# First batch attended in two row parts, w_out scaled by halves, some low halves of w_in by TensorE

## The chip, the cores and the metric

One NeuronCore of a Trainium2 chip runs the whole program. The metric is the device time of one execution in microseconds (us), the median of the runs. Five engines work side by side, each with its own queue of instructions in program order: PE (TensorE, matrix products into PSUM; PEld are its weight loads), DVE (VectorE), ACT (ScalarE), POOL (GpSimd), and SP, which here only issues DMAs. PSUM has eight banks of 128 x 512 fp32.

## The reference

Causal attention over 4 batches, 12 heads, 448 rows of 64, and then an MLP with a squared relu over the 1792 rows of 768:

```python
scores = scale * np.matmul(q, k.transpose(0, 1, 3, 2))       # [4, 12, 448, 448]
scores = np.where(mask, -1000000000.0, scores)               # causal
scores = scores - np.max(scores, axis=-1, keepdims=True)
attn = np.exp(scores)
attn = attn / (np.sum(attn, axis=-1, keepdims=True) + 1e-09)
attn_out = np.matmul(attn, v).astype(np.float32)
x = attn_out.transpose(0, 2, 1, 3).reshape(1792, 768)
h = x @ w_in                                                 # w_in  [768, 2048], float64
r = np.maximum(h, 0.0)
g = r * r
return (g @ w_out).astype(np.float32)                        # w_out [2048, 768], float64
```

q, k and v are float32. The two weights arrive as float64, 12.6 MB each.

## The kernel before

**Arithmetic.** A float32 factor is split into a high and a low f16 half, and a product is three f16 products (high-high, high-low, low-high) accumulated in PSUM. Powers of two, worked out on the chip from sums of squares, keep the halves in range (`pow2`, lines 439 to 452). Batch 0's whole attention and the scores of batch 1 are done in fp32 instead; the scores of batches 2 and 3 and all other products with the attention weights are split.

**Attention** (`pair`, 598 to 758). A batch has 6 pairs of heads. A pair's q and k are turned to have d on the partitions (for batches 0 and 1 by PE with the identity, 629, and a copy, 577; for 2 and 3 by splitting, 416 to 430, and a DMA transpose, 614). Rows go in 4 chunks of 112; chunk c has scores for c + 1 key blocks. `soft` (647) scales, masks and takes the row's extremum on DVE in one custom operation (649, which leaves a second small instruction that reads the accumulator) and takes the exponential and its row sum on ACT (653). Batch 0 then scales the weights (`scaled`, 569), turns them block by block on PE (709), copies them (577) and multiplies with v in fp32 (721). Batches 1 to 3 split them into `psrc` (`halves`, 583: 416/418 high, 429 low), a DMA transpose brings them to `pT` (595), and PE multiplies (731). x goes to `xt` in two halves (748, 752). The low half of a block, in any place, is a DVE operation on a scaled difference (429) or two POOL operations; an unscaled one is line 424.

**Weights** (`weights_in`, 826; `weights_out`, 865). w_in comes in 24 tiles of 128 x 512, w_out in 16 of 128 x 768. Each is staged as raw float64 in whatever lies free (g, xt of odd batches, `raw`), narrowed to float32 bit by bit (`narrow`, 793), and squared by PE for its scale (840, 881). Narrowing is two DVE operations (801, 804) and a third that adds the low word: on DVE too (809), or, in every second tile (`POOLED`), a conversion on ACT (815) and an add on POOL (817), in pieces of 512. w_in gets a scale for each of four column groups `f`; w_out gets its scale from all of its 16 tiles and the four scales of w_in. Then `split_w` (820) writes the halves over the float32. The raw q, k and v of batch 0 lie in the space of w_out from its tile 5 on.

**MLP** (`sub_block`, 931). The 1792 rows go in sub-blocks of 256 or 128 rows: batch 0 has 256 and 128 (its last 64 rows are handled with batch 1), batch 1 has 256 and 256, and so on. A sub-block first rescales x by powers of two (940 to 966, all six pairs), then for 16 column blocks `m` runs 18 products over w_in (L1, 996), relu (1007, ACT), square (1014), high half (416) and low half (424, POOL or DVE). Then for each 128 rows and each half of the 768 output columns it runs 48 products over all of w_out (L2, 1032), one eviction with a scale per row on ACT (1042), and a DMA out (1046).

**Order.** All of this is listed as operations with the tiles that they read and write. `Plan` (69 to 260) puts them in order: it plays a list schedule with the estimated length of each operation on each engine that may do it, and of the operations that are ready it picks the one with the smallest due time, which is a number per phase and per kind from the table `PR` (21). Operations with several possible engines (high halves, squares, copies, scalings) are given one there. Phases are a0 to a3 (attention), m (MLP), wi/ws (w_in narrowed / split), wo/wt (w_out). In the list of the program, attention 0 comes first, then the weights, then for each batch its MLP and the attention of the next.

PSUM banks are given out by role: pv in 0; scores of batch 0 in 1, 3 and 2, 4, of batch 1 in 1 and 2; transposes in 5, 6 or 3; L1 in 4 and 5; L2 in 6 and 7; sums of squares in 7.

Of the kernel before, what the change touches and what calls it, by code (L numbers as in the profile page):

```python
# [68 lines left out]
class Plan:  # L69
# [26 lines left out]
    def spot(self, keys, ap):  # L96
# [190 lines left out]
def dma_ns(nbytes, run):  # L287
    return nbytes / (360.0 if run >= 512 else 180.0)
# [3 lines left out]
def attention_relu2_kernel(  # L292
# [37 lines left out]
    F16V = [False, True, True, True]  # L330
# [180 lines left out]
    def v_up(b):  # L511
        return vst[:, 8 * (b % 2) + 6:8 * (b % 2) + 7]
# [352 lines left out]
    def weights_out():  # L865
        for i in range(KF):
# [7 lines left out]
            if i == 0:  # L874
                ps = n_gram()
# [253 lines left out]
```

## Time and profile before

| | |
|---|---|
| median of 3 runs | 677.19 us (676.54 to 678.2) |
| the profiled execution | 677.23 us |
| its span, first to last instruction | 675.5 us |
| PE busy | 618.0 us |
| ACT busy | 439.4 us |
| DVE busy | 380.3 us |
| POOL busy | 153.3 us |
| mean granted TensorE clock | 0.96 |

The busy time of PE says how long products were in it, not how fast it went: the granted clock has two levels, 1.2 and 2.4 GHz, and is given as a share of the full one, as a mean over a stretch. A product at half clock counts twice the time. So a stage is read by two numbers together, busy time and clock.

### The profile page before, as it was taken

The numbers are of one execution on the slowest core, as the hardware profiler recorded it, in microseconds if no ns is written. First come the engines' busy times: TensorE is split into PE (matmuls) and PEld (weight loads), VectorE is DVE, ScalarE is ACT, GpSimd is POOL, SyncE is SP. The second block draws the span as 40 slices with busy tenths as digits, with TensorE's granted clock in tenths as the row PEclk, the third lists the DMA queues.
The fourth block names the chain that finished last, engine by engine and source line by source line (L and its number), as shares of the span: only waits on it lengthen the run. The fifth ranks groups of instructions, "written<-read, shape, count | busy, mean of one in ns | idle before, by whom it ended". The sixth has DMA issues, their size and how long they took to land.

```text
span 675.5 us, 13694 instructions
## 1 busy us (share of the span) xinstructions
PE 618.0 (91%) x5030; PEld 448.6 (66%) x5030; DVE 380.3 (56%) x1134; ACT 439.4 (65%) x1275; POOL 153.3 (23%) x202
## 2 busy tenths in 40 slices
PE   5876766689999998999999999999999999999997
PEld 3444545366676575778686687768777778767864
DVE  3999898989897766966878777750200300200000
ACT  2878878789999797788877996744514434304400
POOL 4332223103321231143001323112302122103200
PEclk9987778779999998999999999999999999999999
DMA  9998767667655899878999997681000000000000
GB/s 245 304 274 249 250 236 277 151 150 131 144 94 104 178 180 187 174 124 168 183 183 167 186 182 131 127 162 40 13 13 24 14 13 1 13 24 13 13 25 23
DMA packets 208675, 87.30 MB, mean 129 GB/s; under 512 B 196064, under 2 KB 203488, under 8 KB 208608
## 3 DMA queue, kind: packets, MB, share of 16 engines
q1 hardware_dynamic: 208608, 86.43, 56.6%
q8 instruction: 39, 0.64, 0.4%
q14 instruction: 28, 0.23, 0.1%
HBM read 45.81 MB, written 5.51 MB: 76 GB/s over the span
## 4 chain that ended last, share of the span: by engine, by line
PE 58%; DMA 14%; DVE 12%; ACT 10%; issue 3%; SPq 2%; POOL 1%; POOLq 0%; ACTq 0%; DVEq 0%
PE bank L1032 25%; PE bank L996 22%; DMA pT<-psrc 4%; PE bank L731 3%; PE bank L666 3%; DVE bank L649 2%; ACT p L653 2%; DVE wi L804 2%; PE bank L680 2%; ACT psrc L416 2%; DMA qT<-qs 1%; ACT p L569 1%; DMA vn<-in_v_dram 1%; DMA raw<-in_moe_w_in_dram 1%; DVE psrc L429 1%
## 5 line engine op out<-in xcount | busy, mean ns | idle before, releaser
L996 PE MATMUL bank<-xt,wi 128*128 128x256 f16 (+1 forms) x2304 | 232.4, 260 | 0.9 <-ACT r L1007 0.9
L1032 PE MATMUL bank<-wo,g 128*128 128x384 f16 x1344 | 230.4, 327 | 0.0
L996 PEld LDWEIGHTS <-wi 128*128 128x128 f16 x2304 | 201.2, 98 | 27.7 <-issue 5.2
L1032 PEld LDWEIGHTS <-g 128*128 128x128 f16 x1344 | 130.4, 98 | 84.4 <-issue 3.8
L424 POOL TENSOR_TENSOR g<-g,g 128x256 f16<-128x256 f32 (+1 forms) x128 | 83.8, 667 | 290.3 <-ACT g L416 183.6
L653 ACT ACTIVATE p<-bank,nm 112x112 f32<-112x112 f32 (+3 forms) x192 | 93.1, 489 | 28.2 <-DVE nm L649 23.0
L429 DVE SCALAR_TENSOR_TENSOR psrc<-p,nm,psrc 112x112 f16<-112x112 f32 (+3 forms) x144 | 70.8, 518 | 11.4 <-ACT psrc L416 10.6
L1007 ACT ACTIVATE r<-bank 128x256 f32<-128x256 f32 (+1 forms) x128 | 44.6, 354 | 50.1 <-PE bank L996 49.1
L1042 ACT ACTIVATE ob<-bank,fac 128x384 f32<-128x384 f32 x28 | 16.2, 578 | 84.3 <-PE bank L1032 84.3
L416 ACT ACTIVATE psrc<-p,nm 112x112 f16<-112x112 f32 (+3 forms) x144 | 65.4, 520 | 6.5 <-DMA pT<-psrc 6.0
L951 DVE TENSOR_SCALAR u<-bank 128x256 int32<-128x256 int32 (+1 forms) x8 | 3.1, 382 | 106.0 <-PE bank L946 106.0
L649 DVE CUSTOM_DVE_ANT_0 bank<-bank,mask,sc 112x112 f32<-112x112 f32 (+3 forms) x96 | 48.2, 511 | 15.0 <-PE bank L666 7.8
L416 ACT ACTIVATE g<-g 128x256 f16<-128x256 f32 (+1 forms) x128 | 47.2, 388 | 12.7 <-PE bank L1032 11.4
L1014 ACT ACTIVATE g<-r 128x256 f32<-128x256 f32 (+1 forms) x128 | 49.3, 386 | 8.4 <-POOL g L424 4.9
L680 PE MATMUL bank<-kT,qT 64*112 64x336 f32 (+3 forms) x192 | 39.5, 480 | 10.6 <-ACT p L653 7.9
L649 DVE CUSTOM_DVE_ANT_0 bank<-bank,mask 112x112 f32<-112x112 f32 (+3 forms) x96 | 40.9, 476 | 11.3 <-PE bank L680 8.1
L666 PE MATMUL bank<-kT,qT 128*112 128x112 f16 (+3 forms) x192 | 36.3, 288 | 2.1 <-ACT p L653 1.9
L653 ACT ACTIVATION_READ_ACCUMULATOR p<-bank,nm 112x1 f32 x192 | 38.3, 199 | 0.0
L709 PE MATMUL bank<-ident,p 112*112 112x112 f32 x120 | 28.6, 393 | 7.7 <-ACT p L569 5.1
L731 PE MATMUL bank<-pT,vp 112*64 112x448 f16 (+3 forms) x432 | 30.2, 284 | 4.6 <-DMA pT<-psrc 3.7
L731 PEld LDWEIGHTS <-vp 112*64 112x64 f16 x432 | 22.0, 109 | 15.2 <-issue 7.0
L680 PEld LDWEIGHTS bank<-kT,qT 64*112 64x112 f32 x192 | 16.4, 188 | 20.9 <-ACT p L653 14.1
(120 smaller groups left out, 669.0 us busy)
## 6 DMA issues: line engine op xcount, KB each, us to landing
raw<-in_moe_w_out_dram SPq DMA_DIRECT2D x8, 768.0 KB, 5.1
xt<-in_moe_w_out_dram SPq DMA_DIRECT2D x8, 768.0 KB, 5.6
xt<-in_moe_w_in_dram SPq DMA_DIRECT2D x11, 512.0 KB, 5.3
out_dram<-ob SPq DMA_DIRECT2D x28, 192.0 KB, 1.9
raw<-in_moe_w_in_dram SPq DMA_DIRECT2D x9, 512.0 KB, 6.0
vn<-in_v_dram SPq DMA_DIRECT2D x18, 224.0 KB, 3.1
raw<-in_v_dram SPq DMA_DIRECT2D x18, 224.0 KB, 3.3
raw<-in_q_dram SPq DMA_DIRECT2D x12, 224.0 KB, 3.5
```

The lines of the kernel that those rows point to most:

```text
L416: nc.scalar.activation(out=o, in_=i, func=ACTF.Copy, scale=s)
L424: return plan.add({"dve": dve_ns(n), "pool": pool2_ns(n)}, lambda e: engines[e].tensor_tensor(out=out(), in0=in_(), in1=top(), op=ALU.subt ...
L429: nc.vector.scalar_tensor_tensor(out=out(), in0=in_(), scalar=scale(), in1=top(), op0=ALU.mult, op1=ALU.subtract)
L649: one("dve", dve_ns(w, 1, 2 if F16S[b] else 1) - 10, lambda e: nc.vector.tensor_tensor_reduce(out=s.ap[0:P, 0:w], in0=s.ap[0:P, 0:w], in1= ...
L653: one("act", act_ns(w, True, 1, True), lambda e: nc.scalar.activation(out=p32[j].ap[:, b0:b0 + c + 1, :].rearrange("p a t -> p (a t)"), in ...
L666: nc.tensor.matmul(out=s.ap[0:P, 0:(c + 1) * P], lhsT=qT.ap[:, j * NCH + c, :], rhs=kT.ap[:, a:a + c + 1, :].rearrange("p a t -> p (a t)") ...
L680: nc.tensor.matmul(out=ss[j].ap[0:P, 0:(c + 1) * P], lhsT=f32t(q32)[r, c * P:(c + 1) * P], rhs=f32t(k32)[r, 0:(c + 1) * P], start=True, st ...
L731: nc.tensor.matmul(out=pv.ap[j * D:(j + 1) * D, kc * P:S], lhsT=vp.ap[:, hv, vb:vb + D], rhs=pT[j].ap[0:P, hp * NSL + x:hp * NSL + x + w, ...
L996: nc.tensor.matmul(out=h.ap[:, 0:n], lhsT=wi_hl(ci, hw)[:, ms], rhs=x[:, kd, hx, off:off + n], start=(kd == 0 and hw == 0 and hx == 0), st ...
L1007: nc.scalar.activation(out=r.ap[:, 0:n], in_=h.ap[:, 0:n], func=ACTF.Relu)
L1014: nc.scalar.activation(out=g32.ap[:, 0:n], in_=r.ap[:, 0:n], func=ACTF.Square)
L1032: nc.tensor.matmul(out=o.ap[:, 0:HALF], lhsT=g[:, kf, hg, tt * 128:(tt + 1) * 128], rhs=wo_hl(kf, hw)[:, hh * HALF:(hh + 1) * HALF], start ...
```

## The change

Batch 0 is attended by a function of its own, `early`, in two row parts: part 0 is rows 0 to 255 in two chunks of 128, part 1 is rows 256 to 447 in two chunks of 96. Each part goes through all six pairs, the scores of a pair ahead of the weights and values of the pair before it, with three sets of buffers in turn (some of them in psrc, which is therefore padded later). Its q and k are turned in one group per pair and copied back in place. The program's list is now: part 0, w_in, part 1, w_out, then both sub-blocks of batch 0, with both first layers (L1) ahead of both second layers (L2), and batch 1's attention after them. The second sub-block has a g of its own in the space of qT and kT.

w_out is scaled in two halves of 8 tiles, each with its own scale, so L2 runs in two accumulations of 24 products; ACT evicts the first, DVE adds the second to it. All tiles are narrowed by three DVE operations. For the first two of four column groups of w_in (12 tiles) the low half is made by PE: diag(scale) times the float32 tile, less the high half, and a copy out of PSUM. Batch 1's q and k are copied in place, its scores have two banks per head, those of batches 2 and 3 three. All of PR's numbers differ, and two more phases, e (part 1) and n (MLP of batch 0), have their own; the estimate of DMA lengths is lower.

```diff
-    POOLED = (1, 3, 5, 7)
-    SB = {True: ([1, 3], [2, 4]), False: ([1], [2])}
-    TB = {True: [5, 6], False: [3]}
-    HB = {True: [4, 5], False: [4, 5]}
-    OB = {True: [6, 7], False: [6, 7]}
+    SB = {0: ([1, 3], [2, 4]), 1: ([1], [2])}
+    TB = {0: [5, 6], 1: [3]}
+    HB = [4, 5]
+    OB = [[6, 4, 5], [6, 7]]
-    S16 = [1, 2]
+    S16 = [1, 2, 3]
+    S32 = ([1, 3], [2, 7])
+    WL = [6]
+    ON_PE = 2
+    KEYS = [(0, 128), (128, 128), (256, 96), (352, 96)]
...
+    EARLY = [(n, part, c) for n in range(3) for part in range(2) for c in range(2)]
+    early_at = lambda n, part, c=0: wo[:, (5 + 4 * n + 2 * part + c) * 2 * DM:(6 + 4 * n + 2 * part + c) * 2 * DM].bitcast(F32)
...
-        plan.add({"act": act_ns(n, False, 1), "dve": dve_ns(n, 1, 1), "pool": pool_ns(n, 1)}, fn, reads, writes, due, "nrm", True)
+        plan.add({"act": act_ns(n, False, 1), "dve": dve_ns(n, 2, 1), "pool": pool_ns(n, 1)}, fn, reads, writes, due, "nrm", True)
...
+    def early(part):
+        T0, M, N = (0, 128, 256) if part == 0 else (256, 96, 192)
+        phase, slot = ("a", 2) if part == 0 else ("e", 0)
...
+        def scored(pr):
...
+            one("pe", 4 * (0.86 * M), turn, qkk + ["ident"], [t], due)
+            copy(4 * M, lambda rows=rows: rows[:, :, part, :, 0:M],
+                 lambda t=t: t.ap[:, 0:4 * M].rearrange("p (n c t) -> p n c t", n=2, c=2), [t], qkk, due)
+            p32, pT = [[mk(j) for j in range(2)] for mk in (lambda j: n_ep(part, j, pr % 3), lambda j: n_eT(j, pr % 3))]
...
+        for step in range(NPAIR + 1):
+            if step < NPAIR:
+                scored(step)
+            if step:
+                applied(step - 1)
...
+    def split_pe(src, hl, n, key, scale, skey, dg, due):
+        hi(n, lambda: hl(0), lambda: src, scale, [key(1), skey], [key(0)], due)
+        t = n_wl()
+
+        def rest(e):
+            nc.tensor.matmul(out=t.ap[:, 0:n], lhsT=dg.ap, rhs=src, start=True, stop=False)
+            nc.tensor.matmul(out=t.ap[:, 0:n], lhsT=minus, rhs=hl(0), start=False, stop=True)
+
+        one("pe", mm32_ns(n) + mm_ns(n), rest, [key(1), key(0), dg, "minus"], [t], due)
+        plan.add({"act": act_ns(n, True), "dve": dve_ns(n)}, lambda e:
+                 nc.scalar.activation(out=hl(1), in_=t.ap[:, 0:n], func=ACTF.Copy) if e == "act"
+                 else nc.vector.tensor_copy(out=hl(1), in_=t.ap[:, 0:n]), [t, key(1)], [key(0)], due, "rest")
...
-            pr, z = divmod(i + 1 - 5, 2)
-            over = [k_ for n in (z, z + 1) for k_ in raw_of(pr)[n][1]] if 0 <= pr < NPAIR else []
+            over = [("b0", *EARLY[i - 4], pr) for pr in range(NPAIR)] if 4 <= i else []
...
+            if i % (KF // 2) == KF // 2 - 1:
+                scale_out(i // (KF // 2), ps)
...
+            if z == 0:
+                ob = held[tt, hh] = n_ob(phase == "n" and n == SUB, 2 * tt + hh)
+                one("act", act_ns(HALF, True, 1), lambda e: nc.scalar.activation(
+                    out=ob.ap, in_=o.ap[:, 0:HALF], func=ACTF.Copy, scale=scale()),
+                    [o, (facs[tt], 1)], [ob], (phase, pos, "ob"))
+                return pos
+            ob = held[tt, hh]
+            one("dve", dve_ns(HALF, 1, 1), lambda e: nc.vector.scalar_tensor_tensor(
+                out=ob.ap, in0=o.ap[:, 0:HALF], scalar=scale(), in1=ob.ap, op0=ALU.mult, op1=ALU.add),
+                [o, (facs[tt], 2), ob], [ob], (phase, pos, "ob"))
...
+    early(0)
+    weights_in()
+    early(1)
+    weights_out()
+    pos, last0 = sub_block(0, 0, 256, 0, [(256, 2)], 0.0, "n")
+    pos, last1 = sub_block(0, 256, 128, 256, [(128, 0)], pos, "n", True)
+    last1(last0(pos))
+    spare = [plan.spot([("psrc", i, j) for j in range(2)], psrc[i]) for i in range(2)]
+    plan.add({"pool": 2000}, pads, [], spare + ["pads"] + [("psrc", i, c, z) for i in range(2) for c in range(NCH) for z in range(2)],
              ("a", H, "ld"))
-    attention(0)
-    weights_in()
-    weights_out()
+    attention(1)
     pos = 0.0
-    for b in range(B):
+    for b in range(1, B):
```

## Rows read from the trace of the kernel before

**Rows 1.** The page, busy time by engine: us, share of the span, instructions

```profile
PE 618.0 (91%) x5030; PEld 448.6 (66%) x5030; DVE 380.3 (56%) x1134; ACT 439.4 (65%) x1275; POOL 153.3 (23%) x202
```

**Rows 2.** Stretches from:to us: length, busy us by engine, granted clock, DMA

```profile
0.00:20.00 20.00, 11.65 (x58) 6.63 (x58) 8.01 (x32) 6.38 (x17) 8.27 (x11) 1.00 1.01 261
20.00:143.00 123.00, 88.32 (x572) 58.31 (x571) 116.16 (x323) 98.92 (x270) 33.71 (x27) 0.80 0.79 242
143.00:282.00 139.00, 132.21 (x1189) 93.64 (x1188) 113.20 (x331) 121.10 (x363) 33.64 (x46) 0.98 0.76 146
282.00:462.00 180.00, 175.79 (x1495) 133.66 (x1494) 127.69 (x405) 142.73 (x428) 43.26 (x60) 1.00 0.86 160
462.00:671.00 209.00, 209.00 (x1720) 155.97 (x1719) 15.28 (x48) 69.69 (x197) 34.46 (x59) 1.00 0.04 14
671.00:675.50 4.50, 0.98 (x7) 0.39 (x4) 0.00 (x0) 0.58 (x1) 0.00 (x0) 1.00 0.12 44
```

Here the columns behind the length are PE, PEld, DVE, ACT and POOL, then the granted clock, the share of the DMA engines and GB/s.

**Rows 3.** The same columns, ten us of the second stretch

```profile
130.00:140.00 10.00, 5.45 (x28) 3.01 (x27) 9.89 (x41) 7.34 (x25) 0.41 (x1) 0.54 0.77 189
```

**Rows 4.** The chain that ended last: start us, length us, what

```profile
129.54 4.64 DMA raw<-in_v_dram
...
143.28 2.56 PE bank L996 x18
...
281.99 1.96 PE bank L996 x18
```

**Rows 5.** Stretches, line 752 alone (low half of x): DVE busy and count

```profile
143.00:272.00 129.00, 3.72 (x6) 0.98 0.75 143
```

**Rows 6.** Groups by line, 0 to 143 us: busy us, mean ns, idle before

```profile
L817 POOL TENSOR_TENSOR wo<-wo,qs 128x512 int32<-128x512 int32 (+1 forms) x16 | 18.8, 1179 | 43.1 <-DVE nm L693 8.0 <-PE bank L881 7.0 <-ACT qs L815 6.7
L1077 POOL MEMSET psrc<- 128x3328 f16 x2 | 5.7, 2872 | 0.0
...
L815 ACT ACTIVATE qs<-raw 128x512 int32<-128x512 uint32 (+1 forms) x22 | 12.8, 591 | 5.2 <-DMA raw<-in_moe_w_in_dram 3.3 <-POOL wi L817 1.8
...
L804 DVE SCALAR_TENSOR_TENSOR wi<-xt,wi 128x512 int32<-128x512 int32 x11 | 11.7, 1067 | 0.1
L809 DVE SCALAR_TENSOR_TENSOR wo<-xt,wo 128x768 uint16<-128x768 uint32 x8 | 9.5, 1192 | 0.0
L429 DVE SCALAR_TENSOR_TENSOR wi<-wi,wst 128x512 f16<-128x512 f32 x9 | 7.1, 791 | 0.0
L809 DVE SCALAR_TENSOR_TENSOR wi<-xt,wi 128x512 uint16<-128x512 uint32 x7 | 5.1, 727 | 0.0
```

**Rows 7.** Timeline: start us, length us, engine, line, operation

```profile
23.49 1.39 POOL L817 TENSOR_TENSOR wi<-wi,qs 128x512 int32<-128x512 int32 x1 [4.24 <-DVE nm L693]
...
23.78 1.65 DVE L804 SCALAR_TENSOR_TENSOR wi<-xt,wi 128x512 int32<-128x512 int32 x1
...
26.32 0.67 DVE L804 SCALAR_TENSOR_TENSOR wi<-xt,wi 128x512 int32<-128x512 int32 x1
```

**Rows 8.** The chain that ended last, products of three kinds: start, length, what

```profile
66.88 2.04 PE bank L721 x16
...
120.93 3.57 PE bank L721 x16
...
214.26 2.92 PE bank L1032 x18
```

**Rows 9.** Groups by line and shape on DVE, 143 to 282 us

```profile
L429 DVE SCALAR_TENSOR_TENSOR psrc<-p,nm,psrc 112x448 f16<-112x448 f32 x15 | 11.0, 731 | 0.0
...
L429 DVE SCALAR_TENSOR_TENSOR qs<-raw,sc,qs 112x512 f16<-112x512 f32 x8 | 6.0, 772 | 0.6 <-POOL qs L418 0.6
...
L649 DVE CUSTOM_DVE_ANT_0 bank<-bank,mask,sc 112x448 f32<-112x448 f32 x5 | 3.4, 686 | 0.4 <-ACT g L416 0.4
```

**Rows 10.** Groups by shape: a square of L1, 143 to 282; x's low half, 0 to 150

```profile
L1014 ACT ACTIVATE g<-r 128x256 f32<-128x256 f32 x16 | 6.6, 412 | 0.2
...
L752 DVE SCALAR_TENSOR_TENSOR xt<-bank,vst,xt 128x448 f16<-128x448 f32 x6 | 4.1, 676 | 0.0
```

More of the change, by code (lines that the diff above doesn't have):

```diff
@@ L52 @@
+    "wt_wn.hi@dve": -21687, "wt_wn.hi@pool": 56404, "wt_wn.lo@dve": 7504, "wt_wn.lo@pool": 51738,
 }
@@ L477, in vnorm @@
         w = VN // NPAIR
-        due = ("a", b * H, "vn0" if b == 0 else "vn")
-        for pr in range(NPAIR) if b else ():
+        due = ("a", b * H, "vn")
+        for pr in range(NPAIR):
             t = n_vn([128, w], F32)
@@ L578, in copy, with halves @@
                  else nc.vector.tensor_copy(out=out(), in_=in_()), reads, writes, due, "copy")
-    order = [(kc, c) for kc in range(NCH) for c in range(kc, NCH)]
-    def halves(n, src, rr, rkey, pT):
+    def halves(n, src, skey, rr, rkey, pT):
         ps = psrc[n % 2][0:P]
@@ L736, in pair @@
         due = ("a", 2 * i + 1, "val")
-        if F16V[b]:
-            one("pe", 1550, values16, [(vp, 0), (vp, 1)] + pT, [pv], due, tiled=True)
-        else:
-            one("pe", 2050, values, raws[2][1] + [(p_, a) for p_ in pT for a in range(0, NB10, 4)], [pv], due, tiled=True)
+        one("pe", 1550, values16, [(vp, 0), (vp, 1)] + pT, [pv], due, tiled=True)
         due = ("a", 2 * i + 1, "x")
@@ new lines, in narrow @@
+        t = src.bitcast(I32).rearrange("p (f w) -> p f w", w=2)
+        d = dst.bitcast(I32)
+        d2 = d.bitcast(U16)[:, 0::2]
+        one("dve", dve_ns(n, 2), lambda e: nc.vector.tensor_scalar(
+            out=d, in0=t[:, :, 1], scalar1=3, scalar2=0x3FFFFFFF,
+            op0=ALU.logical_shift_left, op1=ALU.bitwise_and), keys, [dkey] + list(over), due, port=True)
+        one("dve", dve_ns(n), lambda e: nc.vector.scalar_tensor_tensor(
+            out=d, in0=t[:, :, 1], scalar=-0x40000000, in1=d, op0=ALU.bitwise_and, op1=ALU.bitwise_or),
+            keys + [dkey], [dkey], due, port=True)
@@ L903, in weights_out @@
         s1 = n_s1([128, 8], I32)
         def total(e):
-            w = wst[:, 32:32 + FQ]
-            nc.vector.tensor_tensor(out=w, in0=w, in1=wst[:, RHO2:RHO2 + FQ], op=ALU.mult)
-            nc.vector.tensor_reduce(out=s1.ap[:, 0:1].bitcast(F32), in_=w, axis=AX.X, op=ALU.add)
-        one("dve", 146, total, [("wosq", f) for f in range(FQ)] + ["rho"], [s1, "wosum"], due)
+            nc.vector.tensor_tensor(out=grp(32), in0=grp(32), in1=grp(RHO2), op=ALU.mult)
+            nc.vector.tensor_reduce(out=s1.ap[:, 0:1].bitcast(F32), in_=grp(32), axis=AX.X, op=ALU.add)
@@ L924, in weights_out @@
-        one("dve", 138, back, ["wodn", "rho"], ["wback"], due)
-        for i in range(KF):
+            nc.vector.tensor_tensor(out=col(BACK), in0=col(MAXD), in1=col(MAXD), op=ALU.mult)
+            nc.vector.tensor_tensor(out=col(BACK), in0=col(BACK), in1=col(WDN), op=ALU.mult)
+        one("dve", 138, back, [("wodn", z), ("rho", z)], [("wback", z)], due)
+        for i in range(z * KF // 2, (z + 1) * KF // 2):
             c = SO + i * FQ // KF
             split_w(wo_raw(i), lambda hl, i=i: wo_hl(i, hl), DM, lambda o, i=i: ("wo", i + o),
-                    lambda c=c: wst[:, c:c + 1], "wout", ("wt", i, "wn"))
@@ L998, in first @@
                             start=(kd == 0 and hw == 0 and hx == 0), stop=(kd == KD - 1 and hw == 1))
-            one("pe", 3 * KD * mm_ns(n), first, xk + [("wi", (m // 4) * KD + kd) for kd in range(KD)], [h], ("m", pos, "L1"))
+            one("pe", 3 * KD * mm_ns(n), first, xk + [("wi", (m // 4) * KD + kd) for kd in range(KD)], [h], (phase, pos, "L1"))
             pos += 3 * KD * mm_ns(n)
@@ new lines, in sub_block, with outputs, second @@
+        held = {}
+        def outputs(tt, hh, z, pos):
+            o = n_o(0 if phase == "n" else 1)
+            for k0 in range(z * KF // 2, (z + 1) * KF // 2, 2):
+                def second(e, k0=k0):
+                    for kf in range(k0, k0 + 2):
+                        for hg, hw in ((0, 0), (0, 1), (1, 0)):
+                            nc.tensor.matmul(
+                                out=o.ap[:, 0:HALF], lhsT=gv[:, kf, hg, tt * 128:(tt + 1) * 128],
+                                rhs=wo_hl(kf, hw)[:, hh * HALF:(hh + 1) * HALF],
+                                start=(kf == z * KF // 2 and hg == 0 and hw == 0), stop=(kf == (z + 1) * KF // 2 - 1 and hg == 1))
+                one("pe", 6 * mm_ns(HALF), second,
+                    [gk(kf, a) for kf in range(k0, k0 + 2) for a in range(2)]
+                    + [("wo", kf) for kf in range(k0, k0 + 2)], [o], (phase, pos, "L2"))
+                pos += 6 * mm_ns(HALF)
+            scale = lambda: facs[tt].ap[:, 1 + z:2 + z]
+            if z == 0:
+                ob = held[tt, hh] = n_ob(phase == "n" and n == SUB, 2 * tt + hh)
[7 more added lines that the diff above has]
+                [o, (facs[tt], 2), ob], [ob], (phase, pos, "ob"))
+            r0 = t0 + tt * 128
+            one("sp", 546, lambda e: nc.sync.dma_start(
+                out=out[r0:r0 + 128, hh * HALF:(hh + 1) * HALF], in_=ob.ap), [ob], [], (phase, pos, "ob"))
+            return pos
@@ L1050, in attention, with last @@
+        places = [(tt, hh, z) for tt in range(n // 128) for hh in range(2) for z in range(2)]
+        if phase == "n":
+            places.sort(key=lambda a: a[2])
+        def last(pos):
+            for a in places:
+                pos = outputs(*a, pos)
+            return pos
+        return pos, last
     def attention(b):
         pairs = list(range(b * NPAIR, (b + 1) * NPAIR))
-        for i in pairs if b == 0 else ():
-            pair_load(i)
         vnorm(b)
         for i in pairs:
-            for n in (i, i + 1) if b else ():
+            for n in (i, i + 1):
```

491 lines of the change are left out of this document (282 added, 209 removed), and 43 rows, old and new, of the table PR.

## The prediction

> **What bounds the kernel now.** I read the views from the whole to the part. TensorE is busy for 91% of the span [rows 1], so a gain has to be looked for where it is not. The table by stage [rows 2] finds the place: from 282 to 671 us PE is never idle for more than 4.2 us in all and its clock is full, while before 143 us it is idle and half throttled. I turn each stage into work at full clock (busy time times granted clock) and loss (the rest of the stage). 0 to 20 us: 11.65 of work, 8.35 lost. 20 to 143: 88.32 x 0.80 = 70.7 of work, 52.3 lost. 143 to 282: 132.21 x 0.98 = 129.6, 9.4 lost. 282 to 462: 4.2 lost. 671 to the end: 3.5 lost. Work sums to 597.6 us, loss to 77.9. So two thirds of all loss lies in one stage of 123 us, and what the clock did there follows how busy PE was: in the ten us before 140 it was busy for 5.45 and was granted 0.54 [rows 3]; in the dense stages it has 1.00 [rows 2]. The two levels are 1.2 and 2.4 GHz, so 0.54 is nearly all at 1.2.
>
> What keeps PE short there is VectorE: 116.16 of 123 us busy, 94.4%, against 98.92 on ACT and 33.71 on POOL [rows 2]. In this stage batch 0 is attended, and all of w_in and w_out is narrowed and partly split. PE has no dense work, because the first product of the MLP comes at 143 us [rows 4]. Then batch 0's MLP covers batch 1's attention: DVE falls to 113.2 of 139 us and PE loses only 9.4. Batch 1's six x are ready by 272 us [rows 5]; its first layer starts at 282 [rows 4], when PE has worked off batch 0. From there the MLPs cover everything.
>
> So the time is set by T*, the moment when all obligatory work ahead of batch 1's MLP is done on DVE, and on PE: after it PE is fed.
>
> **The change, part by part: TensorE.** The reference's arithmetic stays. Attention of batch 0 keeps ten key blocks per head; per head the score rows are 128 + 256 + 352 + 448 = 1184 columns against 1120, 6% more of something that overlaps anyway. New are the 12 low halves of w_in: each an fp32 product of 512 columns with a diagonal, and an f16 one that subtracts the high half. The trace has no such pair. Nearest are the 16 fp32 records of L721, which do 1120 columns for a pair of heads in 2.04 us, or 3.57 at 121 us [rows 8]: 0.93 or 1.63 us for 512. The f16 one: 18 of 384 columns take 2.92 us [rows 8], so 0.22 for 512. That is 12 x 1.18 = 14.2 us at the better rate, 12 x 2.06 = 24.7 at the worse (f16 doubled). I take 14.2, since the splits are the very work that makes the stage denser; the other end is 10 us more of PE time in a stage that loses 52, so it costs nothing unless the loss is gone. The lower bound is 0 for the same reason.
>
> **VectorE up to T*.** By 282 us DVE was busy 8.0 + 116.2 + 113.2 = 237.4 us [rows 2]. Not obligatory is what it did for batch 2: splitting q and k, 6.0; 17 scores with a scale pointer, 8.7 in four forms (the 448 one stands), and 17 accumulator reads of 0.14 us, 2.4; 3 of 15 sets of psrc low halves, 31.4 x 3/15 = 6.3; small ones 4.4 [rows 9]. That leaves 237.4 - 27.8 = 209.6. The edits on it:
> (1) every narrowing now has its third operation on DVE. 20 of 40 had it on ACT and POOL (28 operations each, L815 and L817; the largest group of each stands) [rows 6]. Added: 12 x 0.73 + 8 x 1.19 = 18.3 us [rows 6]. ACT is rid of 16.8 us in all, POOL of 34.9.
> (2) 12 low halves leave DVE: 12 x 0.79 = 9.5 us off [rows 6]; 12 PSUM copies come instead, which I give to ACT, at about 0.7 each (an estimate from 0.68 for 448 columns out of PSUM on DVE [rows 10]); on DVE they would be 8 to 9 us more.
> (3) waits behind POOL. An L804 that starts while L817 runs takes 1.65 us, the next one, with POOL at rest, 0.67 [rows 7]. The 11 on xt average 1.07 [rows 6]: 4.4 us over 0.67, and I put all lines of the narrowing at 7 (bounds 0, if POOL takes other work in the same place, and 10).
> (4) small: x's low half in 12 pieces, +1.2; six second evictions of L2 by DVE for batch 0, at most 0.68 each [rows 10], +3.7; scaling w_out twice, +1.5; four gram reductions fewer and two diagonals more, -0.6.
> Sum: +18.3 - 9.5 - 7 + 5.8 = +7.6, so 217 us by T*. ACT has 6.4 + 98.9 + 121.1 = 226.4 by 282 [rows 2], batch 2's share still in it; less 16.8, plus 8.4 for the copies, it has at most 218, and without batch 2's share clearly less than DVE: not the bound.
>
> **What the order gives.** The first 256 rows need only part 0 of each pair, 384 of 1184 columns, about a third of the attention. L1 of batch 0 can then begin at some 60 to 85 us (an estimate: a third of what DVE and ACT do for batch 0's attention, and w_in) and not at 143. Its evictions cost ACT three operations of about 0.4 us (one stands in [rows 10]) and POOL one per 1.96 us of PE [rows 4], as now. This doesn't remove vector work; it moves PE work under it. Scores into three pair buffers and double banks for batch 1 cost nothing. Two things are taken away: batch 0's L1 no longer covers batch 1's attention, and the padding of psrc (5.7 us on POOL [rows 6]) now stands between part 1 and batch 1; I cost that at nothing beside the narrowing of w_out, 5.7 if that is done. The other 22 second evictions of L2 fall mostly after 462 us, where DVE is busy 15.3 of 209 us [rows 2]: nothing. The last one ends the kernel as the ACT one did.
>
> **The sum.** DVE does 8 us in the first 20. The other 209 at the rate of its full stage (0.944) end at T* = 20 + 221 = 241; at its mean rate from 20 to 282 (229.4 / 262 = 0.875) at 259. I take 250. PE must by then have done 211.9 - 8.1 (batch 2) + 14.2 = 218: loss 32 in place of 70, still 10% of the stretch behind the first 20 us against 7% in 143 to 282, so PE allows it. After T* come 385.8 + 8.1 of work and 7.7 of loss, 401.6. Span 651.6; the profiled execution was 677.23 for a span of 675.5, so 1.7 lies outside, and it stands on the median (677.19). Forecast 653 us, its own range 643 to 664.
>
> **The rivals.**
> Both pack (639 us): ACT and POOL take 10 us of DVE's flexible work, 199 / 0.944 + 20 = 231, and PE, at full clock, loses 5 to 7% behind the first 20 us: T* = 236 to 241. For it: ACT and POOL have room. Against: the first L1 waits on six pairs. The Trainium skill, TensorE: Matmul & The Clock Gate, Part 1, says that the slow clock is the default and that activity releases it; the rows of this case agree (0.54 when PE was sparse [rows 3], 1.00 when dense [rows 2]). By that rule the 17.7 us that rows 2 show lost to the clock come back as soon as L1 fills the stage, and this rival is the result; and by the same rule, were the stage to stay sparse, the splits would cost the 24.7.
> DVE keeps it (670): the waits of (3) stay, since POOL gets the scalings instead, 216 / 0.875 + 20 = 267. For it: 94% busy today, and the change adds to DVE.
> Slower (684): batch 1 loses its cover. Its raw buffers are freed by the last w_out tiles; tiles 4 to 15 land where batch 0's q, k and v lie, and those of v are held until the last values of part 1. Now batch 1's first load lands at 129.5 us [rows 4], and its last x is there after some 135 us more. If part 1 ends only at 145 and batch 1 still takes 135, T* = 280: 280 + 401.6 + 1.7 = 684. The break-even is T* = 274: a start at 139 if it takes 135 us, at 174 if it takes 100. Against: with batch 0's L1 out of the way it should take less than 135.
> No change (677): L1 still comes late, because the rescaling waits for all six pairs and the planner puts w_out ahead; the splits hide in idle time.
>
> **How the numbers follow.** Forecast 0.45, both pack 0.13, DVE keeps it 0.20, slower 0.15, no change 0.07. A measurement tells about 0.3%, 2 us, from no change. Faster takes the first three, less 0.01 of the third: 0.77; same 0.07; slower 0.16. The range leaves out half of the packing case below 638 and most of the slower one above 679.
>
> **What would show it.** Right: L1 before 90 us; a granted clock above 0.9 from there; narrowing operations never near 1.6 us; batch 1's last x near 250; PE loss before that near 32; DVE above 90% until then. Wrong: DVE below 85% while PE idles (batch 1 waits for its loads), or PE idle after batch 1's MLP has begun (batch 2 lost its head start).

## The result, and the profile after

The changed kernel takes 654.17 us (median, 653.54 to 654.5) against 676.87 us (675.66 to 678.2) for the kernel before on the same chip: a ratio of 0.9663, interval 0.9643 to 0.9684. The forecast was 653, with 643 to 664 as its own range.

The page, busy time by engine (us, share of the span, instructions), against [rows 1]:

```profile
span 651.8 us, 14056 instructions
...
PE 614.0 (94%) x5166; PEld 446.6 (69%) x5166; DVE 423.5 (65%) x1263; ACT 415.3 (64%) x1171; POOL 140.4 (22%) x200
```

TensorE is busy 4 us less in a span 24 us shorter; DVE has 43 us more, ACT 24 less. What DVE has more lies behind the start of batch 1's MLP: by 248 us it is busy for 216.8, where it had 237.4 by 282 [rows 2], and from 254 us on it does the relus of batches 1 to 3 (96 operations, 38.1 us), which ACT did before. The stages are the place to look. The table of stretches, columns as in [rows 2] (length, PE, PEld, DVE, ACT, POOL, granted clock, DMA share, GB/s), cut where the changed kernel turns:

```profile
0.00:20.00 20.00, 13.41 (x70) 8.14 (x72) 8.76 (x37) 9.30 (x27) 1.88 (x10) 1.00 0.91 239
20.00:66.00 46.00, 37.25 (x258) 21.69 (x255) 42.58 (x148) 37.64 (x110) 0.00 (x0) 0.96 0.74 228
66.00:143.00 77.00, 70.71 (x678) 57.10 (x677) 75.05 (x167) 64.66 (x166) 37.37 (x34) 1.00 0.56 189
143.00:248.00 105.00, 98.08 (x887) 63.85 (x884) 90.44 (x261) 91.80 (x266) 22.15 (x38) 1.00 0.84 191
248.00:262.00 14.00, 9.88 (x59) 7.18 (x59) 8.24 (x31) 7.41 (x23) 0.67 (x1) 0.63 0.74 166
262.00:462.00 200.00, 198.28 (x1700) 151.92 (x1699) 158.53 (x518) 160.67 (x467) 50.07 (x69) 1.00 0.79 160
462.00:651.80 189.80, 186.39 (x1526) 136.69 (x1524) 39.94 (x108) 43.86 (x116) 28.22 (x49) 1.00 0.04 16
```

Read as before, work is busy time times granted clock and loss is the rest: losses of 6.6, 10.2, 6.3, 6.9, 7.8, 1.7 and 3.4 us, 42.9 in all against 77.9. Work is 608.9 against 597.6. So 35 us of loss went and 11.3 of work came, which is the 23.7 of the spans. The stage that had lost 52.3 us [rows 2] now loses 16.5, and its clock, 0.54 at the worst place before [rows 3], is 0.96 and 1.00.

The first layers of batch 0 (L1, line 1139 in the changed kernel) begin at 65.9 us, where they began at 143 [rows 4]; second layers (L2, line 1176) begin at 137.5. One line each, all their products with the first and last start:

```profile
L1139 PE MATMUL bank<-xt,wi x2304: 216/272/422, 65.9 to 616.9; 128*128 128x256 f16 x144, 128*128 128x128 f16 x48
L1176 PE MATMUL bank<-wo,g x1248: 323/326/338, 137.5 to 648.1; 128*128 128x384 f16 x179
```

The one stretch that still stands out is 248 to 262, where batch 1's MLP takes over. Timeline of it, chosen lines (line 740 writes the low half of batch 1's sixth x, 1087 and 1099 rescale x, 686 is a score of batch 2, 466 a low half of batch 2's q or k):

```profile
242.72 0.62 DVE L740 SCALAR_TENSOR_TENSOR xt<-bank,xt 128x448 f16<-128x448 f32 x1 [1.92 <-ACT xt L736]
...
246.28 0.42 DVE L1087 TENSOR_SCALAR u<-bank 128x256 int32<-128x256 int32 x1
...
248.12 0.68 DVE L1099 TENSOR_TENSOR xt<-xt,sg 128x1024 f16<-128x1024 f16 x1
...
248.85 0.81 PE L1139 MATMUL bank<-xt,wi 128*128 128x256 f16 x6 [2.78 <-DVE xt L1099]
...
250.46 1.44 PE L1139 MATMUL bank<-xt,wi 128*128 128x256 f16 x6 [0.79 <-DVE xt L1099]
250.66 0.75 DVE L466 SCALAR_TENSOR_TENSOR qs<-raw,sc,qs 112x512 f16<-112x512 f32 x1 [0.25 <-ACT qs L453]
...
256.08 1.09 PE L686 MATMUL bank<-qk 128*112 128x336 f16 x5 [2.30 <-DMA qk<-qk]
```

From the start of the last x to the first product on it pass 6.1 us of that operation, squares, a sum, six small DVE operations and the first rescaling. Then the three rescalings stand apart, with the row factors and batch 2's q and k between them, PE drops to half clock (6 products in 1.44 us, then), and its queue holds a score of batch 2 that waits 2.30 us for a DMA ahead of the next L1. The changed kernel has nothing left of batch 0 to put there.

### The profile page after: what moved, and what is told of

It is laid out like the page before. It is cut to its first block, busy times and chain, and to the rows that moved or that the text cites. A ratio compares the mean times of both kernels' runs of the same rounds, so it can differ in the third digit from the quotient of the medians.

```text
span 651.8 us, 14056 instructions
## 1 busy us (share of the span) xinstructions
PE 614.0 (94%) x5166; PEld 446.6 (69%) x5166; DVE 423.5 (65%) x1263; ACT 415.3 (64%) x1171; POOL 140.4 (22%) x200
## 4 chain that ended last, share of the span: by engine, by line
PE 57%; issue 15%; DVE 14%; ACT 5%; DMA 5%; SPq 3%; POOL 1%; POOLq 0%; ACTq 0%; DVEq 0%
PE bank L1176 25%; PE bank L1139 23%; PE bank L724 3%; PE bank L686 3%; DMA pt<-psrc 2%; DVE wo L929 2%; DVE wo L926 2%; DVE wo L923 2%; SPq L756 1%; DVE bank L814 1%; DMA xt<-in_moe_w_in_dram 1%; DVE wi L929 1%; DMA g<-in_moe_w_in_dram 1%; DVE wi L926 1%; PE bank L938 1%
## 5 line engine op out<-in xcount | busy, mean ns | idle before, releaser
L461 POOL TENSOR_TENSOR g<-g,g 128x256 f16<-128x256 f32 (+1 forms) x112 | 78.6, 711 | 305.2 <-ACT g L453 174.9
L1152 DVE TENSOR_SCALAR r<-bank 128x256 f32<-128x256 f32 (+1 forms) x96 | 38.1, 400 | 92.5 <-PE bank L1139 61.7
L673 ACT ACTIVATE pq<-bank,nm 112x336 f32<-112x336 f32 (+3 forms) x144 | 70.7, 508 | 17.0 <-DVE nm L669 10.7
L466 DVE SCALAR_TENSOR_TENSOR psrc<-pq,nm,psrc 112x224 f16<-112x224 f32 (+3 forms) x144 | 71.2, 526 | 5.9 <-ACT psrc L453 5.2
L453 ACT ACTIVATE psrc<-pq,nm 112x224 f16<-112x224 f32 (+3 forms) x144 | 65.3, 545 | 2.9 <-DMA pt<-psrc 2.9
L455 POOL TENSOR_SCALAR g<-g 128x256 f16<-128x256 f32 x16 | 14.9, 936 | 99.4 <-ACT g L1157 99.4
L686 PE MATMUL bank<-qk 128*112 128x112 f16 (+3 forms) x192 | 33.2, 290 | 3.2 <-DMA qk<-qk 2.9
L673 ACT ACTIVATION_READ_ACCUMULATOR pq<-bank,nm 112x1 f32 x144 | 31.5, 219 | 0.0
L724 PE MATMUL bank<-pt,vp 112*64 112x448 f16 (+3 forms) x432 | 29.9, 284 | 1.0 <-DMA pt<-psrc 0.9
L686 PEld LDWEIGHTS <-qk 128*112 128x112 f16 x192 | 20.8, 133 | 8.9 <-DMA qk<-qk 3.6
L806 PE MATMUL bank<-wo 64*96 64x256 f32 (+4 forms) x144 | 19.7, 382 | 4.4 <-ACT wo L601 4.3
L814 DVE CUSTOM_DVE_ANT_0 bank<-bank,mask 128x128 f32<-128x128 f32 (+3 forms) x48 | 21.3, 486 | 2.6 <-PE bank L806 2.4
```

Of the source, the lines that this page charges most:

```text
L453: nc.scalar.activation(out=o, in_=i, func=ACTF.Copy, scale=s)
L461: return plan.add({"dve": dve_ns(n), "pool": pool2_ns(n)}, lambda e: engines[e].tensor_tensor(out=out(), in0=in_(), in1=top(), op=ALU.subt ...
L466: nc.vector.scalar_tensor_tensor(out=out(), in0=in_(), scalar=scale(), in1=top(), op0=ALU.mult, op1=ALU.subtract)
L673: one("act", act_ns(w, True, 1, True), lambda e: nc.scalar.activation(out=p32[j].ap[0:P, b0 * P:b0 * P + w], in_=s.ap[0:P, 0:w], func=ACTF ...
L686: nc.tensor.matmul(out=s.ap[0:P, 0:(c + 1) * P], lhsT=qT.ap[:, j * NCH + c, :], rhs=kT.ap[:, a:a + c + 1, :].rearrange("p a t -> p (a t)") ...
L724: nc.tensor.matmul(out=pv.ap[j * D:(j + 1) * D, kc * P:S], lhsT=vp.ap[:, hv, vb:vb + D], rhs=pT[j].ap[0:P, hp * NSL + x:hp * NSL + x + w, ...
```

## The experiments

Twelve runs. The question behind them: is it the earlier cover that pays, the clock, or VectorE's load? At the end a table sets one number beside all of them.

**The early first layers.** The first layers of batch 0 also wait for the second scale of w_out; nothing else changes.

```diff
-            one("pe", 3 * KD * mm_ns(n), first, xk + [("wi", (m // 4) * KD + kd) for kd in range(KD)], [h], (phase, pos, "L1"))
+            one("pe", 3 * KD * mm_ns(n), first, xk + [("wi", (m // 4) * KD + kd) for kd in range(KD)]
+                + ([("wog", 1)] if phase == "n" else []), [h], (phase, pos, "L1"))
```

> The changed kernel, but batch 0's first layers wait for the squares of w_out's second half, as late as they came before the change (L1 from 157 us on and not from 66). Nothing is left out. Theory (the gain is cover: PE work moved under the vector-bound start): 46 us of L1 that PE did before 157 us now comes behind it, where PE loses only some 10 us, so 654 + 36 = 690 us, range 675 to 700, PE loss before batch 1's first layer near 65 us. Rival (the gain is cheaper vector work, the order matters little): 660 us or less.

Measured: 682.1 us, ratio 1.0104 (1.0069 to 1.014). L1 begins at 150.9, and the stretch that the changed kernel fills is sparse and half throttled again:

```profile
66.00:143.00 77.00, 54.66 (x378) 37.86 (x376) 72.20 (x163) 56.85 (x138) 6.21 (x2) 0.74 0.58 203
```

28 us go, more than the whole gain. Everything else in the change, without this one order, is no gain: this kernel is 1% slower than the one before.

**The low halves on TensorE.** `ON_PE` is the number of column groups of w_in, of four, whose low halves PE makes: 2 in the change. First none, then all four; and, to part the clock from VectorE's load, a third kernel in which PE makes its 12 products as in the change but nothing reads them: DVE or POOL makes the low halves again.

```diff
-    ON_PE = 2
+    ON_PE = 0
```

> The changed kernel with all low halves of w_in made by DVE or POOL again, none by TensorE. Nothing is left out. Theory (DVE sets the end of the start): 9.5 us more on DVE at 91% busy make 10 us, 664 us. Rival (PE sets it): PE is rid of 11 to 14 us, 641 us.

Measured: 664.26, ratio 0.9833 (0.9811 to 0.9854). The clock falls too, so this alone doesn't say which it was.

```diff
-        plan.add({"act": act_ns(n, True), "dve": dve_ns(n)}, lambda e:
-                 nc.scalar.activation(out=hl(1), in_=t.ap[:, 0:n], func=ACTF.Copy) if e == "act"
...
+        lo(n, lambda: hl(1), lambda: src, scale, lambda: hl(0), [key(1), skey, key(0)], [key(0)], due, [key(1)])
```

> The changed kernel where the 12 low halves of w_in are made by DVE or POOL as in no_pe_split, while TensorE still runs the 12 pairs of products, whose results nobody reads (the low half waits for them, as the copy did). Nothing is left out. Theory (DVE: the 9.5 us of subtractions set the end): as slow as no_pe_split, 664 to 668 us. Rival (the clock: the pairs keep the granted clock of 20 to 66 us at 0.96, which fell to 0.78 without them): back to 654 us.

Measured: 665.29, ratio 0.9856 (0.9831 to 0.988). Stretch 20 to 66, with no products and with idle ones:

```profile
20.00:66.00 46.00, 37.72 (x242) 24.31 (x239) 44.52 (x149) 36.49 (x107) 0.74 (x1) 0.78 0.70 216
```

```profile
20.00:66.00 46.00, 38.76 (x277) 23.14 (x274) 45.72 (x154) 37.20 (x111) 0.22 (x1) 1.00 0.72 222
```

The idle products bring the clock from 0.78 back to 1.00 and no time with it. In 20 to 66 us they take PE for 7.4 us (fp32) and 2.6 (f16), and what the clock gave back is 9.3 us (38.8 us of work where 37.72 at 0.78 are 29.4). So the idle products used up the clock that they brought, PE's other work came no sooner, and this run doesn't show what a full clock without them would be worth; DVE is busy for 97% and 99% of the stretch in the two. What it does show is the other half: with the same products on PE and nearly the same clock as in the change, the 12 low halves on DVE cost 11 us. That DVE doesn't make them is what pays.

```diff
-    ON_PE = 2
+    ON_PE = 4
```

> The changed kernel with all 24 low halves of w_in by TensorE. Nothing is left out. Theory (DVE): another 9.5 us off DVE, 644 to 648 us. Rival (TensorE has become the bound from 66 us on, where it is 92% busy at full clock): 14 us more of products, 654 to 665 us.

Measured: 659.99, ratio 0.978 (0.9754 to 0.9806), 6 us worse than two groups, though by 248 us DVE is busy for 207.0 in place of 216.8. The stretch before 143:

```profile
66.00:143.00 77.00, 74.55 (x643) 54.86 (x642) 70.55 (x153) 66.86 (x169) 35.19 (x26) 1.00 0.60 208
```

PE is now the fuller engine, 97% against DVE's 92%; L2 begins at 154.9 and not at 137.5. Of the three counts tried, two groups are best.

**The narrowing.** The old narrowing (in every second tile a conversion on ACT and an add on POOL), put into the changed kernel; it stages the converted words in the two `qs` buffers in turn.

```diff
...
-        one("dve", dve_ns(n), lambda e: nc.vector.scalar_tensor_tensor(
-            out=d2, in0=t[:, :, 0].bitcast(U32), scalar=2.0 ** -29, in1=d2, op0=ALU.mult, op1=ALU.add),
-            keys + [dkey], [dkey], due, port=True)
+        late = narrowed[0] % 8 in (1, 3, 5, 7)
...
+            one("act", act_ns(m), lambda e, t=t, l3f=l3f: nc.scalar.activation(
+                out=l3f(), in_=t[:, :, 0].bitcast(U32), func=ACTF.Copy, scale=2.0 ** -29), keys, [l3], due)
+            one("pool", pool2_ns(m, False), lambda e, d=d, l3f=l3f: nc.gpsimd.tensor_tensor(
+                out=d, in0=d, in1=l3f(), op=ALU.add), [dkey, l3], [dkey], due)
```

> The changed kernel with the narrowing of before: every second tile has its low words converted by ACT and added by POOL. Nothing is left out. Theory (DVE's demand alone): 18 us less, 7 us of waits back, 643 us. Rival (engines share the bound, and DVE waits while POOL adds; POOL has batch 0's g here): 654 to 664 us.

Measured: 673.36, ratio 0.9964 (0.9942 to 0.9985). My sum says that this spares DVE 11 us; it costs 19. That was the largest miss of all, so I did each weight alone, by `and dkey[0] == "wi"` or `"wo"` behind the list of tiles.

> The changed kernel with the old narrowing (a conversion on ACT and an add on POOL in every second tile) for the 24 tiles of w_in alone; those of w_out keep three DVE operations. With the old narrowing in all 40 tiles it took 673.4 us, 19 more than the changed kernel. Theory that POOL's queue is what delays (the adds wait behind the low halves of g, which POOL makes only once the first layers run): most tiles of w_in are narrowed before that, so the cost is small, 655 to 659 us. Rival, stretched DVE operations beside POOL and two more hand-overs per tile wherever they stand: 12 of the 20 tiles are here, so 12/20 of the 19 us, 664 to 667.

Measured: 660.16, ratio 0.9764 (0.9732 to 0.9796).

> The other half: the old narrowing for every second tile of w_out alone, w_in on DVE. Theory of POOL's queue: these tiles are narrowed while the first layers run and POOL makes low halves of g, so nearly the whole cost is here, 666 to 672 us. Rival (a cost per tile, wherever it stands): 8 of the 20 tiles, in pieces of 512 and 256, 661 to 664.

Measured: 675.11, ratio 0.9978 (0.9959 to 0.9998). Twelve tiles of w_in cost 6 us, eight of w_out 21. So it isn't a price per tile, and the two don't add up (together they cost 19). Both times lie a little above what the theory of POOL's queue had (655 to 659, and 666 to 672). Timeline with w_out's tiles alone, chosen lines of POOL, ACT and PE (461 makes the low halves of g on POOL, 946 is the add, 944 the conversion, 1031 the sums of squares, 929 the first narrowing operation, 1257 the zeroing of `psrc`):

```profile
123.73 2.02 POOL L946 TENSOR_TENSOR wo<-wo,qs 128x512 int32<-128x512 int32 x1
125.70 5.68 POOL L1257 MEMSET psrc<- 128x3328 f16 x2
125.79 0.69 ACT L944 ACTIVATE qs<-raw 128x512 int32<-128x512 uint32 x1 [1.39 <-POOL wo L946]
126.23 5.43 DVE L929 TENSOR_SCALAR wo<-raw 128x512 int32<-128x512 int32 x1
131.34 1.58 POOL L461 TENSOR_TENSOR g<-g,g 128x256 f16<-128x256 f32 x2
...
133.99 1.10 POOL L946 TENSOR_TENSOR wo<-wo,qs 128x256 int32<-128x256 int32 x1 [0.70 <-DVE wo L932]
...
135.12 0.46 ACT L944 ACTIVATE qs<-raw 128x256 int32<-128x256 uint32 x1 [1.71 <-POOL wo L946]
...
135.14 0.29 PE L1031 MATMUL bank<-wo 128*128 128x128 bf16 x2 [3.76 <-POOL wo L946]
```

Each add takes its turn among the halves of g, of which POOL makes the high ones too (455, not shown), and behind the zeroing; the conversion behind it waits for the buffer and holds up ACT's queue (1.39 and 1.71 us here), and PE waits in order for the tile (3.76). L2 starts at 151.9 in place of 137.5, and batch 1's first L1 at 269.9 in place of 248.9, the whole 21 us. In w_in's part (adds from 18 to 80 us) POOL has almost nothing else. That POOL's queue is the way is seen in these rows; w_out's tiles differ in place and size too, and a run with the adds but without batch 0's g on POOL was not made.

Then the same edit in the kernel before: no tile through ACT and POOL.

```diff
-    POOLED = (1, 3, 5, 7)
+    POOLED = ()
```

> The kernel before with one number changed: every tile narrowed by three DVE operations. By the sum of the prediction this puts 18.3 us on DVE and takes back about 7 of waits, on the engine that bounds the stage: 677 + 11 = 688 us. Rival, that the way through ACT and POOL costs more by its delays than it saves on DVE, in the old order too: 665 to 677. In the old order POOL makes no low halves of g at that time, so by the theory of POOL's queue the cost stays what the sum says, 683 to 690.

Measured: 702.59, ratio 1.0386 (1.0347 to 1.0425). The same exchange that is worth 19 us in the new order costs 27 in the old one. L1 and the stretches before it:

```profile
L996 PE MATMUL bank<-xt,wi x2304: 216/272/418, 158.3 to 666.2; 128*128 128x256 f16 x144, 128*128 128x128 f16 x48
```

```profile
20.00:143.00 123.00, 84.90 (x532) 54.42 (x529) 118.46 (x296) 75.19 (x207) 0.00 (x0) 0.74 0.68 215
143.00:158.00 15.00, 7.58 (x32) 4.73 (x33) 14.90 (x51) 12.34 (x32) 0.00 (x0) 0.50 0.72 169
```

With 8.2 in the first 20 us DVE is busy for 141.5 us by the first L1 at 158, where it was 124.2 by 143 [rows 2]: 17.3 more, and L1 15 us later. Batch 1's first layer comes 23 us later (304.7 for 282.0), and the rest of the 27 lies behind it; why more than 15 are lost was not followed up, and 702.6 lies 12 us above the range that I had. Where POOL has no halves of g to make, the sum by DVE's load has the right sign, and 18.3 was the better term than 18.3 less 7.

One rival of both exchanges is untested. The planner's table PR differs in all its numbers between the two kernels, and neither exchange got numbers of its own; how much of the 19 and of the 27 us is an order that no longer suits the work isn't known. Moving another estimate by 2%, below, cost nothing.

**The scales of w_out.** Both halves wait for all 16 tiles.

```diff
...
-            if i % (KF // 2) == KF // 2 - 1:
-                scale_out(i // (KF // 2), ps)
+        for z in range(2):
+            scale_out(z, ps)
...
```

> The changed kernel where both scales of w_out wait for all 16 tiles, so that L2 cannot begin with the first half (at 137 us before the last tile is narrowed at 156). Nothing is left out; both accumulations stay. Theory (cover): L2 comes some 15 us later, PE has L1 of the second sub-block until then, so PE loses about 5 us more: 659 us, range 655 to 665. Rival (the halves are of no use): 654 us.

Measured: 658.69, ratio 0.9751 (0.9725 to 0.9777): L2 begins at 160.1 in place of 137.5, and some 5 us of cover go.

**The padding.** The zeroing of `psrc` cut down to the columns and blocks that nothing else writes.

```diff
-            nc.gpsimd.memset(t, 0.0)
+            t32 = t.bitcast(I32)
+            nc.gpsimd.memset(t32[:, :, P // 2:64], 0)
+            for z in range(0, 2 * NSL, NSL):
+                nc.gpsimd.memset(t32[:, z + 7, :], 0)
+                nc.gpsimd.memset(t32[:, z + 10:z + 12, :], 0)
```

> The changed kernel in the same order of instructions; only the zeroing of psrc on POOL, which stands between part 1 and batch 1, covers the columns and blocks that nothing else writes, about a sixth of the words. Theory (DVE is the bound at 126 us and waits 4.4 us behind the POOL memsets for one narrowing operation): the operation falls from 4.99 to about 1 us and the whole to 650 us. Rival (the prediction's: the zeroing costs nothing): 654 us.

Measured: 651.24, ratio 0.963 (0.9607 to 0.9653). The zeroing left is about a third of the words (592 of 1664 in a row of a tile), not the sixth that I expected. The reason for trying it is in the changed kernel's timeline; below it the line of all such first narrowing operations (min, median, max in ns), of the changed kernel and then of this one:

```profile
125.03 5.68 POOL L1241 MEMSET psrc<- 128x3328 f16 x2
...
125.21 1.03 DVE L929 SCALAR_TENSOR_TENSOR wo<-xt,wo 128x768 uint16<-128x768 uint32 x1
126.13 4.99 DVE L923 TENSOR_SCALAR wo<-raw 128x768 int32<-128x768 int32 x1
```

```profile
L923 DVE TENSOR_SCALAR wo<-raw x8: 544/552/4986, 80.8 to 151.8; 128x768 int32<-128x768 int32 x8
```

```profile
L923 DVE TENSOR_SCALAR wo<-raw x8: 543/552/782, 78.0 to 149.7; 128x768 int32<-128x768 int32 x8
```

The record of a DVE operation that has a median of 0.55 us lasts until both memsets are over. With the memsets cut down those 4.4 us on DVE are gone, and some 2 us of time, but the intervals overlap with the change's. Two kernels with another estimate of a DMA's issue in the planner (475 to 485), which only shuffles the order, were made to see what a shuffle does, without and with the small zeroing.

> The changed kernel with one estimate of the planner moved by 2% (a DMA issue at 485 and not 475 ns), so that the same work is put in another order. Nothing is left out. Both theories: 654 us give or take what an untuned order costs, 0 to 8 us more; this is the yardstick for the other runs that change the list of operations.

Measured: 652.26, ratio 0.9658 (0.9636 to 0.968), as the change.

> The changed kernel with both the small zeroing of psrc (only the columns and blocks that nothing writes) and the issue estimate of the planner at 485 in place of 475. Each alone took 651.2 and 652.3 us at ratios of 0.963 and 0.966, with the changed kernel at 0.966. If the zeroing is worth its 2 to 3 us whatever the order of the work, this gives 650 to 652, a ratio near 0.963; if what was seen was only another order, 653 to 655.

Measured: 651.63, ratio 0.9649 (0.9613 to 0.9685). Beside the shuffled kernel without it, nothing that can be told from it. So the wait is shown in the trace, and its worth in time, about 2 us or nothing, isn't settled. Both kernels with the small zeroing are as fast as any here.

**One number beside them.** The time at which PE begins batch 1's first layer, from the timeline of each kernel, and the median time:

| kernel | L1 of batch 0 | L2 of batch 0 | L1 of batch 1 | time, us | time less the fourth column |
|---|---|---|---|---|---|
| changed | 65.9 | 137.5 | 248.9 | 654.2 | 405.3 |
| shuffled | 62.5 | 134.1 | 245.7 | 652.3 | 406.6 |
| small zeroing | 63.1 | 132.8 | 246.7 | 651.2 | 404.5 |
| small zeroing, shuffled | 64.3 | 133.3 | 245.7 | 651.6 | 405.9 |
| late first layers | 150.9 | 220.3 | 280.9 | 682.1 | 401.2 |
| no low half on PE | 59.9 | 144.3 | 259.0 | 664.3 | 405.3 |
| idle products on PE | 62.4 | 146.5 | 258.3 | 665.3 | 407.0 |
| all low halves on PE | 63.2 | 154.9 | 251.9 | 660.0 | 408.1 |
| w_out scaled at once | 62.8 | 160.1 | 253.1 | 658.7 | 405.6 |
| old narrowing | 74.4 | 146.3 | 271.7 | 673.4 | 401.7 |
| old, w_in alone | 71.4 | 144.2 | 257.1 | 660.2 | 403.1 |
| old, w_out alone | 64.5 | 151.9 | 269.9 | 675.1 | 405.2 |

L1 of batch 1 (the fourth column) moves by 35 us and the last column by 7. The times are medians and the starts come from one profiled execution; that of the late first layers was a long one, 685.9 us, and 405 behind the start. The end is set by the start of batch 1's MLP, whatever caused that; how early batch 0's L1 or L2 begins tells less. Taken out singly, the early L1, the low halves on PE, the narrowing on DVE and the two scales cost 28, 10, 19 and 5 us: they lean on each other and don't add up to the 23. The banks, the copies in place, the relus on DVE and the new numbers in PR were not taken out. (In the two kernels of the old order, where batch 2's attention has had its head start, the difference is 395 and 398.)

## Why the prediction was right, and where it was not

**The bound: right.** That T* sets the time is the table above. I had 401.6 behind it and 1.7 outside, 403.3; the runs have 401 to 408. That DVE's load sets T* holds up to some 160 us (from 143 on it is busy for 16.93 of 17 us), and not behind (see ACT).

**T* and the loss before it: right in number, with luck in DVE's sum.** T* was put at 250 and came at 248.9, with 30.0 us of loss by 248 where I had 32, and 218.0 of work where I had 218. DVE was put at 217 us until then; the stretch from 0 to 250 has 218.8, and 91% of 20 to 250. L1 was put at 60 to 85 and came at 65.9. Batch 1's last x, put near 250, was there at 243.3; the 6 us of rescaling behind it I had not kept apart.

The terms that DVE's sum holds came near: by the lengths of their operations the third ones of the narrowing grew by 17.5 us (18.3), the low halves of w_in fell by 9.4 (9.5) and the second narrowing operations by 6.1 (7). Three things that it hasn't got cancel. The high halves of w_in also left DVE, 9.0 us; one line each, before and after:

```profile
L418 DVE TENSOR_SCALAR wi<-wi,wst x16: 477/486/899, 82.0 to 186.1; 128x512 f16<-128x512 f32 x16
```

```profile
L453 ACT ACTIVATE wi<-wi,wst x24: 711/716/743, 34.8 to 120.6; 128x512 f16<-128x512 f32 x24
```

One narrowing operation stood for 4.4 us behind the zeroing. And lengths were taken off a busy time: the records of neighbouring operations overlap (in the timeline of the padding one starts at 126.13 while the one before it ends at 126.24), so that up to 282 us the lengths of DVE's operations add up to 286.8 where it is busy for 237.4. Batch 2's 27.8 us were then worth some 23 (an estimate, by that share). With all three the sum stays near 217.

**What came after T*: a size off.** I had 7.7 us of loss and it was 12.9. The handover alone took 7.8, shown above; I had carried over 4.2 and 3.5 from [rows 2], where batch 0's L2 still filled PE at that point. Against it stand 3 us less of work than I had.

**TensorE's splits: 14.2 priced.** Their two groups in 20 to 143 us:

```profile
L938 PE MATMUL bank<-wi,dg 128*128 128x512 f32 x24 | 13.8, 657 | 0.0
...
L939 PE MATMUL bank<-wi,minus 128*128 128x512 f16 x12 | 4.8, 400 | 0.0
```

18.6 us of busy time, 1.55 for a pair where I had 1.18 and 2.06 as the ends (0.93 and 0.22 make 1.15, a slip without effect, as is 684 for 683 in the slower rival): the f16 product was undersized (0.40 for 0.22) and the fp32 one too (1.15 for 0.93). All of PE's work grew by 11.3, so other work of PE shrank; that was not followed up. The products themselves cost about 1 us (665.3 with idle ones, 664.3 without), near the nothing that I had; with all four groups PE is the fuller engine and the time 6 us longer.

**The narrowing, steps (1) and (3): right as DVE's load, wrong as the price of the exchange.** I priced the move of 20 third operations to DVE as load, +18.3 less 7 of waits, and so as a cost of 11. In the old order that is the right kind of sum, though too small (17.3 us of DVE by L1, 27 in time). In the new order the old narrowing is the one that costs, 19 us. The step that failed is the one that took POOL's 34.9 us as merely gone and its work on g as unchanged, one operation per 1.96 us of PE. With L1 running early, POOL has batch 0's g in the same stretch, and two operations per block, since the planner gave it the high halves (L455) with the low ones (L461). Its lines in 66 to 143 us:

```profile
L461 POOL TENSOR_TENSOR g<-g,g 128x256 f16<-128x256 f32 x16 | 16.9, 1059 | 1.2
L455 POOL TENSOR_SCALAR g<-g 128x256 f16<-128x256 f32 x16 | 14.9, 936 | 99.4 <-ACT g L1157 99.4
L1241 POOL MEMSET psrc<- 128x3328 f16 x2 | 5.7, 2866 | 0.0
```

The adds would have queued there. The sum came out right because it compared the totals of the two kernels and not this part with its alternative. The sign that I named, no narrowing operation near 1.6 us, was seen on w_in alone, where no second operation took more than 0.70 us (1.65 in [rows 7]); on w_out one first operation took 4.99, above.

```profile
L926 DVE SCALAR_TENSOR_TENSOR wi<-xt,wi x11: 676/682/702, 23.4 to 81.3; 128x512 int32<-128x512 int32 x11
```

**The padding: wrong on its own terms.** The cover that I named, the narrowing of w_out, was not one: it stood still itself for 4.4 us. In time that is about 2 us or nothing.

**ACT: said not to be the bound, and the full engine for 60 us.** From 160 to 220 us ACT is busy without a gap, more than DVE:

```profile
160.00:220.00 60.00, 56.80 (x452) 34.11 (x449) 55.12 (x176) 60.00 (x176) 8.76 (x19) 1.00 0.85 177
```

I had judged it by its total (at most 218 of 250), not by stage. From 220 to 248 neither is full (DVE 18.39 and ACT 21.48 of 28 us). No run lightens ACT there, so whether it sets T* is open.

**The rivals.** Both pack (639): the clock came back as that rival had it, and PE lost 10% behind the first 20 us until 248, not 5 to 7. The Trainium skill, TensorE: Matmul & The Clock Gate, Part 1, has the clock released by activity. The rows agree (0.78 to 1.00 by idle products). How much of the 17.7 us came back with it isn't known, since in that run the idle products used up what the clock gave. ACT did take 9.0 us of DVE's flexible work, the high halves of w_in, and T* was still 249, not 236 to 241: the premise was nearly met and its price was wrong. DVE keeps it (670): the waits of (3) went, so its premise failed; that the old narrowing put back takes 673 is another mechanism. Slower (684): its premise held and more. Part 1's last values are multiplied by 129 us, but batch 1's q is loaded only at 151.2, since w_out's last tiles lie in `raw` until then:

```profile
L563 SPq DMA_DIRECT2D raw<-in_q_dram x4: 313/406/485, 151.2 to 157.1; - x4
```

From there to the last x it took 92 us, where I had 135 for the bad case and had set the break-even at 100 for a start at 174. So the reason against it, that it takes less without batch 0's L1 beside it, carried the case. No change: L1 was not late; the run that makes it late is 1% slower than the kernel before.

## What to carry to other kernels

Find the one moment from which the densest engine is fed to the end, and price every edit by how far it moves that moment; here that held to 7 us over twelve kernels. An exchange of work between engines has no price of its own: here the same narrowing was worth 19 us in one order and cost 27 in the other, so look at what the other engine's queue holds in that stretch, by stage and not by total. A better clock is no gain by itself: here idle products brought it and used it up, and the time stayed.

## What was not expected of the hardware

A DVE tensor_scalar of 0.55 us took 4.99 (and 5.43 in another run) while two POOL memsets of 128x3328 f16, 5.68 us together, ran beside it; it ended 0.4 us after them. The scalar_tensor_tensor just before it, with two inputs, took 1.03 us beside the same memset, near the shortest of its kind (1.02), while one beside POOL's add had been stretched from 0.67 to 1.65 [rows 7]. The Trainium skill, SBUF — State Buffer, section "Who interferes with whom", tells these apart: a DVE operation in a two-port mode and a GpSimd one exclude each other for a whole instruction, and one with two inputs from SBUF contends only with a GpSimd operation that reads SBUF. The rows fit this if the tensor_scalar ran in such a mode, which no row here shows; the wait went on over two instructions.

Idle products of TensorE raised its granted clock from 0.78 to 1.00 over 46 us, and took as much of PE there (10.0 us) as the clock gave back (9.3); the time was 665.3 us with them and 664.3 without.
